# Batch 3's mirrored rows of the second transform read backwards from the same PSUM banks, their residual and output rows reversed through DRAM

## The chip, the core and the metric

The kernel runs on one core of one Trainium2 chip. The metric is the device time of one execution in microseconds. The core has five instruction streams that run side by side and wait for each other by semaphores: TensorE (PE, matrix products into eight PSUM banks), VectorE (DVE), ScalarE (ACT), GpSimd (POOL) and SyncE (SP), which issues most of the transfers. Transfers run on 16 DMA engines.

## The reference

Two layers after one another. The first is a linear attention with decay, step by step over 768 positions; the second mixes the result with a two-dimensional Fourier transform and puts a normalised two-layer network behind it.

```python
# attention, per batch and head: state (48 x 48)
y[t]  = r[t] @ (state + u * k[t] v[t]^T)
state = w[t] * state + k[t] v[t]^T
# x: (4, 768, 384), heads side by side
X  = fft(fft(x, axis=1), axis=2)
u  = x + real(X)
un = (u - mean(u)) / sqrt(var(u) + 1e-6)
out = u + relu(un @ w_ch1) @ w_ch2        # 384 -> 1536 -> 384
```

## The kernel before, in words

There are four batches, each of six chunks of 128 positions. The work of a batch has two parts.

`attention(b, c)` handles a chunk. Four inputs (w, k, r, v) come in 192 KB loads with seven buffers each; the logarithm of w is summed by two products (L773, L777), r and k are scaled, transposed (on TensorE for the first 18 chunks, by a DMA transposition for batch 3), multiplied (L843), masked on VectorE (L848), and the product with v and the state (L893) gives the chunk's rows `x`, which VectorE adds up at L908 into `X`. `fold(b, c)` adds and subtracts mirrored chunks and columns, for the first transform.

`mix(b)` holds the rest. The first transform is done with cosine and sine tables in three products (j = 0, 2, 1; 24 short matmuls of 193 columns from batch 1 on, L968), whose results are moved to `HCS`. Since a real transform is symmetric, only positions 0 to 384 stand in `HCS`; `HCR` (L976 to L983) is a copy of it, reversed and with signs, for positions 385 to 767. The second transform (L989 to L993) makes six blocks `kb` of 128 rows and 384 columns: three matmuls a block, blocks 0 to 2 with weights from `HCS`, blocks 3 to 5 from `HCR`, all against the table `DTM`. VectorE adds the residual `x` and sums the rows (L997) into `UF`; ScalarE or VectorE writes the shifted rows `UN`, ScalarE sums their squares for the variance. For batches 2 and 3 a DMA transposition, issued by SyncE (L1033), turns three blocks of `UN` into `UNT`, one transposition for each half `hf` of a batch (blocks 0 to 2, blocks 3 to 5).

The network then runs half by half: twelve first-layer tiles (three matmuls of 384 columns, L1056) with a relu on ScalarE or VectorE into `HT`, then for each block three second-layer groups of four matmuls (L1075). VectorE scales by the deviation and adds `UF` (L1081) into one of three buffers `OSB`, and SyncE writes it to the output (L1085). The last block of the last batch is cut into 256 and 128 columns, so that its end is short.

The order of the work is written out by hand: `ORDER` holds for each engine the list of operation numbers in which it works, and with them also which engine does an operation that could run on several. Each engine works strictly in its list's order; an operation that waits holds up all behind it on its engine. That is true of SyncE too, whose waits precede its transfers. `schedule` gives each tile its PSUM bank from the lists; `emit` derives the semaphore waits. Numbers such as 1252 or 1299 below are these operation numbers; 1252 is the last attention product of batch 3 in both kernels. Operations below 1259 are the same in both; those of batch 3's `mix` are numbered anew. TensorE's list has 36 matmuls without use (L1130) in the first 37 us.

Of the kernel before, what the change touches and what calls it, by code (L numbers as in the profile page):

```python
# [7 lines left out]
ALU = mybir.AluOpType  # L8
# [28 lines left out]
MEANS = (0, 1, 2, 3)  # L37
# [29 lines left out]
    "act": (  # L67
# [14 lines left out]
    "dve": (  # L82
# [14 lines left out]
    "pool": (  # L97
# [12 lines left out]
}  # L110


class _Tile:


    __slots__ = ("bank", "ops", "pool", "n_done", "end")
# [1047 lines left out]
```

## Time and profile before

| | us |
|---|---|
| median of three runs | 183.09 (182.17 to 183.48) |
| the profiled execution | 184.21 |
| its span, first to last instruction | 182.4 |
| TensorE busy in it | 176.8 |
| VectorE, ScalarE, GpSimd busy | 148.2, 130.2, 101.5 |

The granted clock of TensorE is 1.000 in the whole span. Busy times of TensorE overlap: a 384-column matmul is shown with about 326 ns, while the next one can begin half of that later, so its share of busy time says little of how much of it is used. The chain of waits (what released the work that ended last, step by step) shows the real pitch. A row of the timeline gives the start, the duration, the engine, the line, the operation, the tile written and those read, and in brackets how long the engine had been idle and who released it. A row of waits gives the sum, the count and the longest. The rows of DMA groups give the size and the time from issue to landing. In the rows of "DMA" and "GB/s" a stretch is cut into 40 slices; a digit is the mean busy share of the 16 engines in tenths.

### The profile page before, as it was taken

The page shows a single profiled execution, that of the slowest core. Times are in us where ns is not written, and L with a number is a line of the kernel's source. Part 1 is how long each engine was busy: PE and PEld are TensorE (multiplying, and loading weights), DVE is VectorE, ACT ScalarE, POOL GpSimd, SP SyncE. Part 2 cuts the span into 40 slices and gives each one's busy share as a digit, 9 for nine tenths or more (in the row PEclk, how much of TensorE's full clock was granted, in tenths as well). Part 3 has the DMA queues.
Part 4 walks back from the last instruction along what each step waited for, and adds up shares of the span by engine and source line. Part 5 has one row for each costly group of instructions (what it writes and reads, how often), then busy time and mean ns, then how long its engine had stood idle before and what let it go on. Part 6 is the DMA issues. An engine that isn't in the chain of part 4 may idle for free.

```text
span 182.4 us, 4568 instructions
## 1 busy us (share of the span) xinstructions
PE 176.8 (97%) x1722; PEld 116.3 (64%) x1722; DVE 148.2 (81%) x341; ACT 130.2 (71%) x340; POOL 101.5 (56%) x120
## 2 busy tenths in 40 slices
PE   7999999999999999999999999999999999999994
PEld 3465676766566666776657666656666676666663
DVE  8779999899899999999888997899979927622343
ACT  2889859597898675799899978888882247478200
POOL 2448789767231498589998968769653440000000
DMA  4999998999999899999999999997550103331214
GB/s 97 203 216 196 208 191 172 185 202 208 152 196 190 162 210 230 226 204 182 202 222 218 219 177 207 220 212 179 103 114 0 47 2 65 73 125 43 86 71 145
DMA packets 116119, 28.99 MB, mean 159 GB/s; under 512 B 111361, under 2 KB 116098, under 8 KB 116098
## 3 DMA queue, kind: packets, MB, share of 16 engines
q1 hardware_dynamic: 114514, 26.36, 70.2%
q0 software_dynamic: 1584, 2.36, 8.0%
q8 instruction: 13, 0.21, 0.5%
q14 instruction: 8, 0.07, 0.1%
HBM read 23.59 MB, written 4.72 MB: 155 GB/s over the span
## 4 chain that ended last, share of the span: by engine, by line
PE 61%; DVE 17%; DMA 9%; SPq 4%; ACT 4%; issue 3%; DVEq 0%
PE bank L1075 18%; PE bank L1056 17%; DMA in_w<-in_w_dram 5%; DMA w<-in_moe_w_ch_dram 4%; DVE ah L848 4%; SPq L609 4%; PE bank L992 3%; PE bank L1130 3%; PE bank L1098 3%; PE bank L968 3%; DVE osb L1081 2%; PE bank L843 2%; DVE rkh L561 2%; PE bank L889 2%; PE bank L899 2%
## 5 line engine op out<-in xcount | busy, mean ns | idle before, releaser
L1075 PE MATMUL bank<-w,ht 128*128 128x384 bf16 (+2 forms) x300 | 53.7, 320 | 0.0
L1056 PE MATMUL bank<-unt,w 128*128 128x384 bf16 x288 | 51.9, 326 | 0.6 <-DMA w<-in_moe_w_ch_dram 0.6
L1064 ACT ACTIVATE ht<-bank 128x384 bf16<-128x384 f32 x72 | 32.6, 496 | 9.3 <-PE bank L1056 8.9
L1056 PEld LDWEIGHTS bank<-unt,w 128*128 128x128 bf16 x288 | 26.9, 98 | 17.5 <-DVE ht L1062 0.8
L1075 PEld LDWEIGHTS bank<-w,ht 128*128 128x128 bf16 x300 | 27.5, 98 | 15.2
L848 DVE TENSOR_TENSOR ah<-bank,msk 128x512 bf16<-128x512 f32 x48 | 31.2, 682 | 2.1 <-PE bank L843 2.0
L561 POOL TENSOR_TENSOR rk<-rk,ub 128x384 f32<-128x384 f32 x21 | 21.6, 1034 | 8.6 <-DVE rk L561 7.0
L561 POOL TENSOR_TENSOR vtd<-in_v,dc 128x384 f32<-128x384 f32 x20 | 16.7, 837 | 11.2 <-DVE dc L800 8.1
L1081 DVE SCALAR_TENSOR_TENSOR osb<-bank,rstd,uf 128x384 f32<-128x384 f32 (+2 forms) x25 | 14.8, 596 | 9.5 <-PE bank L1075 5.9
L1062 DVE TENSOR_SCALAR ht<-bank 128x384 bf16<-128x384 f32 x24 | 13.0, 549 | 6.9 <-PE bank L1056 6.8
L561 POOL TENSOR_TENSOR rk<-in_r,in_k 128x384 f32<-128x384 f32 x17 | 16.9, 999 | 2.9 <-DMA in_r<-in_r_dram 1.4
L997 DVE SCALAR_TENSOR_TENSOR uf<-bank,x 128x384 f32<-128x384 f32 x24 | 12.5, 553 | 4.7 <-PE bank L992 4.6
L561 POOL TENSOR_TENSOR rkh<-in_k,e 128x384 bf16<-128x384 f32 x14 | 14.1, 1009 | 3.6 <-ACT e L792 2.0
L779 ACT ACTIVATE bank<-bank 128x384 f32<-128x384 f32 x24 | 11.5, 484 | 5.8 <-PE bank L773 5.8
L811 DVE TENSOR_TENSOR rkh<-bank,in_r 128x384 bf16<-128x384 f32 x24 | 13.1, 549 | 2.1 <-ACT bank L779 2.0
L575 ACT ACTIVATE xf<-uf,agg 128x384 bf16<-128x384 f32 x24 | 14.7, 614 | 0.0
L561 POOL TENSOR_TENSOR xf<-sd 128x382 bf16<-128x382 f32 (+1 forms) x10 | 10.6, 1062 | 6.5 <-DVE sd L561 3.0
L575 ACT ACTIVATE lb<-in_w 128x384 bf16<-128x384 f32 x24 | 12.4, 519 | 2.1 <-DMA in_w<-in_w_dram 1.8
L575 ACT ACTIVATE un<-uf,agg 128x384 bf16<-128x384 f32 x18 | 10.6, 611 | 4.1 <-DVE uf L997 4.1
L586 ACT ACTIVATE rkt<-bank 128x256 f32<-128x256 f32 x29 | 10.8, 389 | 3.6 <-PE bank L833 2.4
L561 POOL TENSOR_TENSOR sd<-x 128x385 f32<-128x385 f32 x10 | 10.0, 1015 | 5.9 <-DVE x L908 5.4
L792 ACT ACTIVATE e<-bank 128x392 f32<-128x392 f32 (+1 forms) x24 | 11.7, 497 | 2.3 <-DVE bank L877 1.0
(138 smaller groups left out, 358.7 us busy)
## 6 DMA issues: line engine op xcount, KB each, us to landing
in_w<-in_w_dram SPq DMA_DIRECT2D x24, 192.0 KB, 3.8
in_k<-in_k_dram SPq DMA_DIRECT2D x24, 192.0 KB, 3.8
in_r<-in_r_dram SPq DMA_DIRECT2D x24, 192.0 KB, 4.1
in_v<-in_v_dram SPq DMA_DIRECT2D x24, 192.0 KB, 4.0
out_dram<-osb SPq DMA_DIRECT2D x23, 192.0 KB, 2.8
w<-in_moe_w_ch_dram POOLq DMA_DIRECT2D x2, 576.0 KB, 8.1
w<-in_moe_w_ch_dram POOLq DMA_DIRECT2D x1, 1152.0 KB, 10.7
out_dram<-osb SPq DMA_DIRECT2D x1, 128.0 KB, 1.7
```

Of the source, the lines that this page charges most:

```text
L561: return lambda e: e.tensor_tensor(out=o, in0=a, in1=b, op=f)
L575: return lambda e: e.activation(o, a, f, **kw)
L779: op("act", a_ps(DM) + 20, lambda e: e.activation(ps(tce)[:, 0:DM], ps(tce)[:, 0:DM], ACTF.Exp), w=[tce])
L792: op("act", a_ps(ne), lambda e: e.activation(E2[i2][:, 0:ne], ps(tci)[:, 0:ne], ACTF.Exp), r=[tci], w=[("E2", i2)])
L811: op("dve", v_1(DM), lambda e: e.tensor_tensor(out=rh[:, :, 0:D], in0=ps(tce)[:, 0:DM].rearrange("t (h d) -> t h d", d=D), in1=rt[:, :, :] ...
L848: masked[n] = op("dve", v_1(512), lambda e, x=x: e.tensor_tensor(out=ah[:, x:H:2, :], in0=ps(ta[x])[:, :].rearrange("p (h t) -> p h t", t= ...
L997: op("dve", v_1(DM) + 60, lambda e, kb=kb, t=t: e.scalar_tensor_tensor(out=uf[:, kb, :], in0=ps(t)[:, 0:DM], scalar=1.0, in1=xb[:, kb, 0:D ...
L1056: ins = e.matmul(ps(t)[:, 0:384], W1[:, m, 256 * (j // 2) + j % 2:256 * (j // 2) + 256:2], unt[:, :, m, :], start=(m == 0), stop=(m == NM ...
L1062: {"dve": lambda e, j=j, t=t, ht=ht: e.tensor_scalar(out=ht[:, j, :], in0=ps(t)[:, 0:384], scalar1=su, scalar2=0.0, op0=ALU.mult, op1=ALU. ...
L1064: "act": lambda e, j=j, t=t, ht=ht: e.activation(ht[:, j, :], ps(t)[:, 0:384], ACTF.Relu, scale=su)},
L1075: ins = e.matmul(ps(t)[:, 0:hi - lo], ht[:, j, 128 * x:128 * x + 128], W2[:, j, lo:hi], start=(j == 0), stop=(j == NJ - 1))
L1081: op("dve", v_1(hi - lo) + 64, lambda e, kb=kb, t=t, o=o, lo=lo, hi=hi: e.scalar_tensor_tensor(out=o[:, lo:hi], in0=ps(t)[:, 0:hi - lo], s ...
```

## The change

For batch 3 (`MIRROR = (3,)`) no `HCR` is made and blocks 3 to 5 have no matmuls of their own. The tile of block 0 serves block 3 too, that of block 1 block 4, that of block 2 block 5: VectorE reads the bank a second time with the columns backwards (384 to 1). `DTM` and the tiles are one column wider for this (385). The rows come out in mirrored order of positions, so two things are reversed through DRAM:

- The residual rows of chunks 3 to 5 are written to a scratch tensor `XD` in DRAM (four transfers, each chunk twice, one copy behind the other) and read back in reversed row order into `UF` (three transfers, 192 KB each). The addition for blocks 3 to 5 then takes `UF` in place of `x`.
- The output rows of blocks 3 to 5 go from `OSB` to a scratch tensor `OD` in two pieces, swapped, and from there in reversed row order to the output (a third transfer each, DRAM to DRAM). Two single rows go out by themselves.

Position 384, which has no mirror, is made by two matmuls with one column of weights and an addition on one partition, into row 0 of block 3.

The blocks are taken in the order 0, 3, 1, 4, 2, 5, and the network does the second half (blocks 3 to 5) first in its numbering, with the buffers `UN` and `UNT` swapped accordingly. All five lists of `ORDER` are new, for all batches. In TensorE's list four first-layer tiles of half 0 come ahead of those of half 1; in VectorE's list operation 1299 (block 3's addition) comes ahead of the other additions of batch 3; the last block on TensorE is block 1, uncut; the cut block is block 2. In `load_one` only the planned cost of a load is altered. The branch for kernels without `MEANS`, which no batch took, is gone.

Core of the diff:

```diff
+MIRROR = (3,)
...
+    def move(fn, r, w, sem, xfer):
+        op("sp", 620, fn, r=r, w=w, sem=sem, xfer=xfer, dma=(1150, 600))
+
+    def back(x, a):
+        return x[a - 63:a + 577, :].rearrange("(z p) d -> z p d", z=2)[:, 63::-1, :]
...
-        for kb in range(NC):
+        if b in MIRROR:
+            xd = XD[b][0:S, :].rearrange("(z c p) d -> z p c d", p=128, z=2)
+            for z in range(2):
+                move(lambda e, z=z: e.dma_start(xd[z, :, 0:2, :], xb[:, 3:5, 0:DM]), [("X", i, 3), ("X", i, 4)], [("XD", b, z, 0)],
+                     "xa%d%d" % (i, z), 1040)
+                move(lambda e, z=z: e.dma_start(xd[z, :, 2, :], xb[:, 5, 0:DM]), [("X", i, 5)], [("XD", b, z, 1)], "xb%d%d" % (i, z), 520)
+            for q in (1, 2, 0):
+                move(lambda e, q=q: e.dma_start(uf[:, NP + q, :], back(XD[b], 384 - 128 * q)),
+                     [("XD", b, z, y) for z in range(2) for y in range(2)], [("UF", i, NP + q)], "xz%d" % q, 520)
+        for kb in (0, 3, 1, 4, 2, 5) if b in MIRROR else range(NC):
...
+            op("dve", v_1(DM) + 60, lambda e, kb=kb, t=t, flip=flip: e.scalar_tensor_tensor(
+                out=uf[:, kb, :], in0=ps(t)[:, DM:0:-1] if flip else ps(t)[:, 0:DM], scalar=1.0,
+                in1=uf[:, kb, :] if flip else xb[:, kb, 0:DM], op0=ALU.mult, op1=ALU.add,
+                accum_out=agg[:, kb, 0:1]), r=[t, ("UF" if flip else "X", i, kb)], w=[("UF", i, kb), ("SUM", i, kb)])
...
+                    move(lambda e, o=o, od=od, m=m, nh=nh: e.dma_start(od[0:nh, :], o[m:m + nh, :]), done, [("OD", b, mq, 0)],
+                         "oa%d" % (n % 3), 260)
+                    move(lambda e, o=o, od=od, m=m, nh=nh: e.dma_start(od[nh:2 * nh, :], o[m - nh:m, :]), done, [("OD", b, mq, 1)],
+                         "ob%d" % (n % 3), 260)
...
+                    t0 = S - 127 - 128 * mq
+                    move(lambda e, od=od, nh=nh, t0=t0: e.dma_start(
+                        out[b, t0:t0 + 2 * nh, :].rearrange("(z p) d -> z p d", z=2),
+                        od[0:2 * nh, :].rearrange("(z p) d -> z p d", z=2)[:, ::-1, :]),
+                         [("OD", b, mq, 0), ("OD", b, mq, 1)], [("out", b, kb, 0)], "fin%d" % mq, 1040)
```

Here `nh` is 63 for block 3 and 64 for blocks 4 and 5.

More of the change, by code (lines that the diff above doesn't have):

```diff
@@ L292, in schedule @@
                 hw.append([s + o.set, o.xfer, o, t])
-                if o.xfer == 960:
+                if o.xfer in (920, 1030):
                     lds.append(o)
@@ L395, in run @@
                 for s in dcount:
-                    if s.startswith("out"):
+                    if s[:3] in ("out", "fin", "oc0", "oc1"):
                         eng.wait_ge(sems[s], dcount[s])
@@ L492, in bass_rwkv6_finch__then__fnet_fourier_mix_kernel @@
     UF = [sb("uf%d" % i, [NC, DM], FP32) for i in range(2)]
-    BST = [sb("bst%d" % i, [6], FP32) for i in range(4)]
     AGG = [sb("agg%d" % i, [NC, 2], FP32) for i in range(2)]
@@ L506, in bass_rwkv6_finch__then__fnet_fourier_mix_kernel @@
     SS = sb("ss", [NP, 2 * HE], BF16)
+    XD = {b: nc.dram_tensor("xd%d" % b, (1024, DM), FP32, kind="Internal").ap() for b in MIRROR}
+    OD = {b: nc.dram_tensor("od%d" % b, (S - S // 2, DM), FP32, kind="Internal").ap() for b in MIRROR}
     CN = sb("cn", [NP, HE], BF16)
     SN = sb("sn", [NP, HE], BF16)
-    DTM = sb("dtm", [3, DM], BF16)
+    DTM = sb("dtm", [3, DM + 2], BF16)
     IDW = sb("idw", [384], BF16)
@@ L734, in rows @@
                         idn = (IDW if cos or half else NIDW)[p0:p0 + np_, 128 - sh:256 - sh]
-                        src = tab[:, 0:HE] if half == 0 else tab[:, HE - 2:0:-1]
-                        dst = ps(t)[:, 0:HE] if half == 0 else ps(t)[:, HE:DM]
+                        src = tab[:, 0:HE] if half == 0 else tab[:, HE - 2::-1]
+                        dst = ps(t)[:, 0:HE] if half == 0 else ps(t)[:, HE:DM + 1]
                         ins = e.matmul(dst, idn, src, start=(i == 0), stop=(i == len(moves[j]) - 1))
@@ L984, in mix @@
         agg, lnv, rstd = AGG[i], LNV[i], RSTD[i]
-        su = -1.0 / DM if b in MEANS else -1.0
-        for kb in range(NC):
-            n = b * NC + kb
-            t = g.tile("f")
-            for j in range(3):
-                def f(e, j=j, kb=kb, t=t):
-                    a = 128 * (kb % NP)
-                    return e.matmul(ps(t)[:, 0:DM], (hcs if kb < NP else HCR)[:, j, a:a + 128], DTM[:, j, :], start=(j == 0), stop=(j == 2))
-                op("pe", mm(DM), f, r=[("HCS" if kb < NP else "HCR", j), "DTM%d" % j], w=[t])
-            iu = (2 * b + kb // 3) % len(UN)
-            un = UN[iu][:, kb % 3, :]
-            if b in MEANS:
-                op("dve", v_1(DM) + 60, lambda e, kb=kb, t=t: e.scalar_tensor_tensor(
-                    out=uf[:, kb, :], in0=ps(t)[:, 0:DM], scalar=1.0, in1=xb[:, kb, 0:DM], op0=ALU.mult, op1=ALU.add,
-                    accum_out=agg[:, kb, 0:1]), r=[t, ("X", i, kb)], w=[("UF", i, kb), ("SUM", i, kb)])
-                op(None, {"act": a_sb(DM) + 95, "dve": v_2(DM) + 60},
-                   {"act": act(un, uf[:, kb, :], ACTF.Identity, scale=-float(DM), bias=agg[:, kb, 0:1]),
-                    "dve": ts(un, uf[:, kb, :], -float(DM), agg[:, kb, 0:1], ALU.mult, ALU.add)}, port=("dve",),
-                   r=[("UF", i, kb), ("SUM", i, kb)], w=[("UN", iu, kb % 3)])
-                op("act", a_sb(DM) + 190, act(xf[:, kb, 63:447], uf[:, kb, :], ACTF.Square, scale=-float(DM), bias=agg[:, kb, 0:1],
-                                              accum_out=agg[:, kb, 1:2]),
-                   r=[("UF", i, kb), ("SUM", i, kb)], w=[("AGG", i, kb)] + [(z, i, kb) for z in ("XFe", "XFo", "XFn")])
-            else:
-                op("dve", v_1(DM), lambda e, kb=kb, t=t: e.tensor_tensor(
-                    out=uf[:, kb, :], in0=ps(t)[:, 0:DM], in1=xb[:, kb, 0:DM], op=ALU.add),
-                   r=[t, ("X", i, kb)], w=[("UF", i, kb)])
-                bs = BST[n % 4]
-                op("dve", v_1(DM), lambda e, kb=kb, bs=bs: e.bn_stats(bs[:, :], uf[:, kb, :]),
-                   r=[("UF", i, kb)], w=[("BST", n % 4)])
-                op("dve", 89, lambda e, kb=kb, bs=bs: e.bn_aggr(agg[:, kb, :], bs[:, :]),
-                   r=[("BST", n % 4)], w=[("AGG", i, kb)])
-                op(None, {"act": a_sb(DM) + 95, "dve": v_2(DM) + 60},
-                   {"act": act(un, uf[:, kb, :], ACTF.Identity, scale=-1.0, bias=agg[:, kb, 0:1]),
-                    "dve": ts(un, uf[:, kb, :], agg[:, kb, 0:1], -1.0, ALU.subtract, ALU.mult)}, port=("dve",),
-                   r=[("UF", i, kb), ("AGG", i, kb)], w=[("UN", iu, kb % 3)])
@@ new lines, in mix @@
+        su = -1.0 / DM
+        made = {}
+        place = {x: 1 - x if b in MIRROR else x for x in range(2)}
+        if b in MIRROR:
+            xd = XD[b][0:S, :].rearrange("(z c p) d -> z p c d", p=128, z=2)
[6 more added lines that the diff above has]
+                     [("XD", b, z, y) for z in range(2) for y in range(2)], [("UF", i, NP + q)], "xz%d" % q, 520)
@@ new lines, in mix, with f @@
+        for kb in (0, 3, 1, 4, 2, 5) if b in MIRROR else range(NC):
+            n = b * NC + kb
+            flip = b in MIRROR and kb >= NP
+            if not flip:
+                t = made[kb] = g.tile("f")
+                for j in range(3):
+                    def f(e, j=j, kb=kb, t=t, w=DM + (b in MIRROR)):
+                        a = 128 * (kb % NP)
+                        return e.matmul(ps(t)[:, 0:w], (hcs if kb < NP else HCR)[:, j, a:a + 128], DTM[:, j, 0:w],
+                                        start=(j == 0), stop=(j == 2))
+                    op("pe", mm(DM), f, r=[("HCS" if kb < NP else "HCR", j), "DTM%d" % j], w=[t])
+            t = made[kb % NP if flip else kb]
+            iu = (2 * b + place[kb // 3]) % len(UN)
+            un = UN[iu][:, kb % 3, :]
+            op("dve", v_1(DM) + 60, lambda e, kb=kb, t=t, flip=flip: e.scalar_tensor_tensor(
+                out=uf[:, kb, :], in0=ps(t)[:, DM:0:-1] if flip else ps(t)[:, 0:DM], scalar=1.0,
+                in1=uf[:, kb, :] if flip else xb[:, kb, 0:DM], op0=ALU.mult, op1=ALU.add,
+                accum_out=agg[:, kb, 0:1]), r=[t, ("UF" if flip else "X", i, kb)], w=[("UF", i, kb), ("SUM", i, kb)])
+            if flip and kb == NP:
+                t = g.tile("f")
+                def f(e, t=t):
+                    for j in range(2):
+                        ins = e.matmul(ps(t)[0:1, 0:DM], hcs[:, j, DM:DM + 1], DTM[:, j, 0:DM], start=(j == 0), stop=(j == 1))
+                    return ins
+                op("pe", mm(DM, 2), f, r=[("HCS", j) for j in range(2)] + ["DTM%d" % j for j in range(2)], w=[t])
+                op("dve", v_1(DM) + 60, lambda e, kb=kb, t=t: e.scalar_tensor_tensor(
+                    out=uf[0:1, kb, :], in0=ps(t)[0:1, 0:DM], scalar=1.0, in1=xb[0:1, kb, 0:DM], op0=ALU.mult, op1=ALU.add,
+                    accum_out=agg[0:1, kb, 0:1]), r=[t, ("X", i, kb)], w=[("UF", i, kb), ("SUM", i, kb)])
+            op(None, {"act": a_sb(DM) + 95, "dve": v_2(DM) + 60},
+               {"act": act(un, uf[:, kb, :], ACTF.Identity, scale=-float(DM), bias=agg[:, kb, 0:1]),
+                "dve": ts(un, uf[:, kb, :], -float(DM), agg[:, kb, 0:1], ALU.mult, ALU.add)}, port=("dve",),
+               r=[("UF", i, kb), ("SUM", i, kb)], w=[("UN", iu, kb % 3)])
+            op("act", a_sb(DM) + 190, act(xf[:, kb, 63:447], uf[:, kb, :], ACTF.Square, scale=-float(DM), bias=agg[:, kb, 0:1],
+                                          accum_out=agg[:, kb, 1:2]),
+               r=[("UF", i, kb), ("SUM", i, kb)], w=[("AGG", i, kb)] + [(z, i, kb) for z in ("XFe", "XFo", "XFn")])
@@ L1020, in mix @@
             hf = kb // 3
-            unt = UNT[(2 * b + hf) % 2]
+            unt = UNT[(2 * b + place[hf]) % 2]
             if b < DMA_U:
@@ L1069, in mix @@
                 o = OSB[n % 3]
-                for lo, hi in ((0, DM),) if n < B * NC - 1 else ((0, 256), (256, DM)):
+                for lo, hi in ((0, DM),) if (b, hf, x) != (B - 1, 0 if b in MIRROR else 1, 2) else ((0, 256), (256, DM)):
                     t = g.tile("f")
@@ L1084, in mix @@
                        r=[t, ("RSTD", i, hf), ("UF", i, kb)], w=[("OSB", n % 3, lo)] + ([] if lo else [("OSB", n % 3, 256)]))
-                    op("sp", 620, lambda e, kb=kb, o=o, lo=lo, hi=hi: e.dma_start(
-                        out[b, kb * 128:(kb + 1) * 128, lo:hi], o[:, lo:hi]),
-                       r=[("OSB", n % 3, lo)], w=[("out", b, kb, lo)], sem="out%d" % (n % 3), xfer=520, dma=(1150, 600))
+                    if b not in MIRROR or kb < NP:
+                        move(lambda e, kb=kb, o=o, lo=lo, hi=hi: e.dma_start(out[b, kb * 128:(kb + 1) * 128, lo:hi], o[:, lo:hi]),
+                             [("OSB", n % 3, lo)], [("out", b, kb, lo)], "out%d" % (n % 3), 520)
+                        continue
+                    mq = kb - NP
+                    m = 65 if mq == 0 else 64
+                    nh = 63 if mq == 0 else 64
+                    od = OD[b][128 * mq:128 * mq + 128, :]
+                    done = [("OSB", n % 3, 0)]
+                    move(lambda e, o=o, od=od, m=m, nh=nh: e.dma_start(od[0:nh, :], o[m:m + nh, :]), done, [("OD", b, mq, 0)],
+                         "oa%d" % (n % 3), 260)
+                    move(lambda e, o=o, od=od, m=m, nh=nh: e.dma_start(od[nh:2 * nh, :], o[m - nh:m, :]), done, [("OD", b, mq, 1)],
+                         "ob%d" % (n % 3), 260)
+                    if mq == 0:
+                        move(lambda e, o=o: e.dma_start(out[b, S - 1:S, :], o[1:2, :]), done, [("out", b, S - 1)], "oc0", 30)
+                        move(lambda e, o=o: e.dma_start(out[b, S // 2:S // 2 + 1, :], o[0:1, :]), done, [("out", b, S // 2)],
+                             "oc1", 30)
+                    t0 = S - 127 - 128 * mq
[3 more added lines that the diff above has]
+                         [("OD", b, mq, 0), ("OD", b, mq, 1)], [("out", b, kb, 0)], "fin%d" % mq, 1040)
     g.ctx = "begin"
```

26 lines of the change are left out of this document (11 added, 15 removed), and 128 rows, old and new, of the table ORDER.

## The prediction

> **What bounds the kernel now.** I read the page first, then what TensorE waits for, then the chain that ended last, then the stretch from 138 us to the end in order of time, and last the DMA views of the quiet stretches.
>
> ```profile
> span 182.4 us, 4568 instructions
> ...
> PE 176.8 (97%) x1722; PEld 116.3 (64%) x1722; DVE 148.2 (81%) x341; ACT 130.2 (71%) x340; POOL 101.5 (56%) x120
> ...
> DMA  4999998999999899999999999997550103331214
> ```
>
> ```profile
> PE bank L1098 <- DVE w L572: 1.3, 1, 1.3
> PE bank L1056 <- DMA w<-in_moe_w_ch_dram: 0.6, 1, 0.6
> PE bank L777 <- ACT ht L1064: 0.3, 1, 0.3
> PE bank L833 <- POOL rkh L561: 0.3, 1, 0.3
> PE bank L843 <- ACT ht L1064: 0.2, 1, 0.2
> ```
>
> TensorE waits 2.7 us in all, 1.3 of it before its first instruction. The DMA engines are full for two thirds of the span and nearly idle in the last third. From the chain come the real costs of matmuls, which overlap:
>
> ```profile
> 146.27 0.84 PE bank L968 x10
> ...
> 156.38 7.80 PE bank L1056 x48
> 164.18 0.65 PE bank L1075 x4
> ...
> 173.28 6.54 PE bank L1075 x52
> 179.92 0.35 DVE osb L1081
> ```
>
> A 384-column matmul costs 7.80/48 = 0.1625 us, a group of four 0.65, a first-layer tile (three) 0.49, a 193-column one 0.084. After the last attention product of batch 3 (operation 1252, done at 141.9) the order of before holds 25 first-layer tiles (12.2), 29 second-layer groups (18.85), 18 matmuls of the second transform (2.9), 23 short ones (1.9) and the last block, cut in two (2.0): 37.85 us. 141.9 + 37.85 = 179.8, which is where TensorE stops. So the tail is matmuls end to end: each one removed is time, and each wait put in front of them is time too.
>
> **The removed work.** Nine 384-column matmuls (blocks 3 to 5 of batch 3) go, two come for the one row without a mirror: -7 x 0.1625 = -1.14 us. The lists say where: after 1252 the new order holds one first-layer tile more, one short matmul less and seven 384-column matmuls less: 37.1 us, so -0.73 there and -0.41 earlier. The extra column (385 for 384) is 0.0004 us a matmul. The three reversed copies of batch 3 fall away:
>
> ```profile
> 142.57 0.54 DVE L908 TENSOR_TENSOR x<-bank,vtd 128x384 f32<-128x384 f32 x1
> ...
> 144.14 0.34 SPq L1085 DMA_DIRECT2D out_dram<-osb  x1
> ...
> 144.78 0.55 DVE L561 TENSOR_TENSOR sd<-x 128x385 f32<-128x385 f32 x1
> ...
> 149.09 1.25 POOL L565 TENSOR_SCALAR hcr<-hcs,cp 128x384 bf16<-128x384 bf16 x1 [2.01 <-ACT hcs L586]
> 149.28 0.52 ACT L978 ACTIVATE hcr<-hcs 128x384 bf16<-128x384 bf16 x1
> ...
> 149.92 0.56 DVE L997 SCALAR_TENSOR_TENSOR uf<-bank,x 128x384 f32<-128x384 f32 x1 [3.46 <-PE bank L992]
> 150.40 0.08 DVE L997 DVE_READ_ACCUMULATOR uf<-bank,x 128x1 f32 x1
> 150.41 0.56 DVE L997 SCALAR_TENSOR_TENSOR uf<-bank,x 128x384 f32<-128x384 f32 x1
> ...
> 152.13 6.02 SPq L1033 DMA_TRANSPOSE unt<-un  x2
> ...
> 153.93 0.75 DVE L566 TENSOR_SCALAR un<-uf,agg 128x384 bf16<-128x384 f32 x2
> ```
>
> They run beside matmuls of batch 2, so they count nothing; without that cover the one on GpSimd, 1.25, would have stood in front of blocks 3 to 5. A residual addition (the operation at L997) starts every 0.48 us; reading its bank backwards I take at the same price, since the nearest row with a reversed operand (the fold, L561, 0.55) costs what the straight ones do.
>
> **The new path in the middle.** Residual rows 3 to 5 now go to DRAM and come back reversed. The last, x of chunk 5, is written at 143.1. SyncE then issues two writes of it (0.34 each), waits until they land, and issues three back-reads; behind them in its queue stand an output and both transposes of the normalised rows. On VectorE the first operation that needs a back-read (1299) stands in front of every residual addition and of the normalised rows 0 to 4. So the back-reads gate both transposes, and these gate the first layer of batch 3. Without delay VectorE gets to 1299 at 143.1 + five fold operations (2.5) + six evictions and output rows (3.1): 148.7. From there: four additions, one normalising (0.37), one addition, one normalising: 151.9, first transposition; one addition, one normalising, the row without a mirror (0.48), one normalising: 153.6, second one.
>
> ```profile
> L1033 SPq DMA_TRANSPOSE unt<-un x2: 1278/1284/1289, 152.1 to 156.9; - x2
> ...
> DMA to landing us min/median/max: 3.2/3.2/3.3
> ```
>
> They land at 155.1 and 156.8. TensorE has its other work until 179.15 - 23.4 = 155.75, takes four first-layer tiles of half 0 (1.95), and turns to half 1 at 157.7. The cover is 0.65 and 0.9 us: any lateness of the back-reads beyond that shows in full. The banks of blocks 0 to 2 stay taken until the mirrored addition has read them; with the lists' five other open tiles that is eight, so TensorE gets through batch 2's groups. SyncE issues 24 transfers for batch 3 instead of 9, 15 x 0.34 = 5.1 us, where it had nothing to do; that counts only if one stands ahead of a late one.
>
> **What a back-read costs.** No transfer of before looks like it: all those of 192 KB have 128 rows in their outermost loop. `back` and the final reversal `fin` have two blocks of 64 (63) rows there, each walked backwards. What 192 KB of 1536-byte rows cost in a quiet stretch:
>
> ```profile
> DMA  9993000000000000000000000000000379999982
> GB/s 389 328 369 123 21 0 0 0 0 0 0 0 0 0 0 0 0 0 0 0 0 0 0 0 0 0 0 0 0 0 0 123 266 348 328 369 430 369 307 82
> ...
> out_dram<-osb SPq DMA_DIRECT2D x1, 192.0 KB, 1.9
> ```
>
> ```profile
> 170.00:176.00 6.00, 6.00 (x40) 3.67 (x38) 1.85 (x5) 0.00 (x0) 0.00 (x0) 1.00 0.28 98
> ```
>
> Data flow for about 0.6 us of the 1.9: some 0.8 lie before, 0.4 behind. Three such outputs in 170 to 176 take 0.28 x 6 = 1.68 us of all 16 engines, 0.56 each, 350 GB/s; the best slice shows 430. Bounds for one back-read: all 16 engines, 0.56 us; one engine, 9 us. If the work is dealt out by the outermost loop, a loop of two feeds two engines: 196,608 bytes at 2/16 of 430 to 350 GB/s is 3.66 to 4.48 us, middle 4.03. I take this value: of all that the code shows, the count of two is what sets these transfers apart from the rows quoted, and both blocks lie on one queue with nothing else to divide by.
>
> The Trainium skill, "DMA: Bandwidth & Descriptors", section "Why a DMA increments its semaphore by 16 and not by 1", states the same rule: the engine count is the largest number up to 16 that divides the outermost counts of both sides, and the lowest-numbered engines are used. By it each of these transfers runs on two engines and all on the same two, and the sum would be the one below; by the rows of the ordinary outputs alone it would be 182.5. No run here shows it yet.
>
> **The sum.** Back-reads: writes issued at 143.2 and 143.6, landed at 145.5; first back-read issued 145.6, data 146.4 to 150.4, landed 150.85; the other two on the same engines at 154.9 and 158.9. VectorE: 1299 at 150.85; three waiting additions; 1322 at 154.9; then normalise, add, normalise: 156.6, first transposition, landed 160.0. 1310 at 158.9, then 0.37, 0.48 and 0.37 with its own 0.5: 160.7, second transposition, landed 164.0. TensorE stands from 155.75 to 160.0, works 1.95 us, stands until 164.0, and has 23.4 - 1.95 = 21.5 us left: its end is 185.5, 6.35 later than without the wait.
>
> Then the end. By the new order blocks 3, 5, 4 (in this order on SyncE) are finished 10.1, 7.7 and 5.65 us before TensorE stops; each goes to DRAM in two pieces and from there backwards to the output. The first `fin` is issued about 6.1 us before the stop (SyncE takes block 5's pieces ahead of it), 179.4, data from 180.2; three at 4.03 on the same two engines: 192.3. The ordinary outputs issued behind them need those engines too, three blocks of 0.5: 193.8, landed 194.2.
>
> ```profile
> 178.38 0.62 DVE L1081 SCALAR_TENSOR_TENSOR osb<-bank,rstd,uf 128x384 f32<-128x384 f32 x1 [0.68 <-PE bank L1075]
> ...
> 179.92 0.35 DVE L1081 SCALAR_TENSOR_TENSOR osb<-bank,rstd,uf 128x128 f32<-128x128 f32 x1 [0.19 <-PE bank L1075]
> ```
>
> ```profile
> in_w<-in_w_dram SPq DMA_DIRECT2D x24, 192.0 KB, 3.8
> ...
> out_dram<-osb SPq DMA_DIRECT2D x1, 64.0 KB, 1.6
> ```
>
> Before, the last piece was 128 columns wide, issued at 180.3, landed 181.9, and the span ended 0.5 later. So the new span is 194.7, +12.3. Without slow transfers the new end would still lose 0.55 us: its last block is whole, 0.27 more on VectorE and 0.3 more to land (1.9 for 1.6).
>
> The profiled execution took 184.21 us, 1.8 outside its span; +12.3 makes 196.5. The median is 183.09, 1.1 below that execution, so 195.4, and I forecast 195.5. With 3.66 us a transfer it is 193.1, with 4.48 it is 198.4.
>
> **The new order elsewhere.** All five lists are rearranged; before batch 3's transform the same operations run. Some 30 elementwise operations go from GpSimd to VectorE and 27 back, and the loads swap places, two of chunk 5 (k and r) behind a transposition of chunk 3. Against the rows this can win at most what TensorE now waits beyond its start, 1.4 us, and I take the same as the loss: nothing as the value, 1.4 both ways in the range. It would be hidden by the batch-2 matmuls that wait beside attention; if they run out, the operation after 1252 moves by the whole delay.
>
> **Rivals.** First, and on the other side: the transfers use all 16 engines, or enough of them. The first back-read then lands at 147.5, the others by 148.6, ahead of 148.7; even with the 3.8 us that loads take on a full queue it is 149.4, which the cover holds within 0.1. The reversals at the end land near the stop of TensorE, under the last output. What is left is -1.14 + 0.55 = -0.6: 182.5. It decides from about eight engines on, 1.1 us a transfer. For it speaks that every 192 KB row here is spread wide; against it the outer count. Second: two engines each, but different ones, so that three run side by side. They land from 150.85 to 151.75, the chain is 2.15 late, 1.5 after the cover; the last reversal, issued 2.5 before the stop, lands 2.75 behind it, against 2.6 for the last output. -0.6 + 1.5 + 0.2: 184.2. Nothing in the rows speaks for a rotation of engines. Third, the worst: DRAM to DRAM is slower than SBUF to DRAM; at twice the data time the end grows by 12 more, past 205.
>
> **How the numbers follow.** Same two engines 0.70 (195.5, own range 190 to 203: 3.66 to 4.48 us, 1.4 of order, and the cover or a slower DRAM reversal); different pairs 0.08 (184.2); wide 0.18 (182.5); worse 0.04. From 184.0 to 203.0 the first two are held, 0.78, and the rest is left out. 1% is about what a measurement of this kernel can tell from no change (the three runs spread over 0.7%): 181.3 and 184.9. Faster 0.04 from the wide case with a lucky order, within 0.22 (most of the wide case and the different pairs), slower 0.74.
>
> **What would show it.** The landing time of the back-reads: about 5, 9 and 13 us for the three if they share two engines, 2 if not. A DMA share near 0.12 (2 of 16) from 146 to 159 and again through the end. TensorE's wait on the transposed rows, some 6 us in two pieces between 155 and 164. An end in which TensorE has stopped and SyncE's reversals still run for 8 us. The forecast is wrong if the share in these stretches rises above a half, or if VectorE's 1299 starts near 148.7 with no wait; then what is left is the first rival.

## The result and the profile after

After the change the kernel takes 199.74 us (median of four runs, 199.34 to 200.34), before it 182.8 (four runs). The ratio is 1.093, 95% interval 1.088 to 1.098: slower by 9%. The profiled execution after took 199.5 us with a span of 197.7.

The page of the kernel after, with the slices that answer to those of before:

```profile
span 197.7 us, 4600 instructions
...
PE 178.0 (90%) x1715; PEld 115.5 (58%) x1715; DVE 152.6 (77%) x357; ACT 125.6 (64%) x327; POOL 96.8 (49%) x116
...
PEclk9999999999999999999999999999999957999965
DMA  5999999999998999899995999890502353103123
```

TensorE's busy time grew by 1.2 us although seven matmuls fell away: the clock row dips in slices 33 and 34 (158 to 168 us), where the kernel before has none, and once more at the very end. Now the waits of TensorE and of VectorE (sum, count, longest):

```profile
PE bank L1074 <- DMA unt<-un: 6.0, 1, 6.0
```

```profile
DVE uf L1020 <- DMA uf<-xd: 9.0, 3, 4.3
...
DVE osb L1099 <- DMA out_dram<-osb: 8.6, 2, 8.2
```

TensorE has one new wait, for the transposed rows of batch 3. VectorE waits three times for back-reads and, at the end, 8.2 us for an output buffer. The kernel before has no wait of the first two kinds, and waits 1.2 us in all for output buffers. The middle in order of time (L915 is x of a chunk, L1002 its write to DRAM, L1004 the back-reads, L1020 the residual addition, L1055 the transposition, L1074 the first layer):

```profile
139.73 0.56 DVE L915 TENSOR_TENSOR x<-bank,vtd 128x384 f32<-128x384 f32 x1 [0.45 <-POOL xf L562]
140.32 1.45 SPq L1002 DMA_DIRECT2D xd<-x  x2
143.37 3.07 SPq L1004 DMA_DIRECT2D uf<-xd  x3
149.81 3.74 PE L1093 MATMUL bank<-w,ht 128*128 128x384 bf16 x22
150.01 0.56 DVE L1020 SCALAR_TENSOR_TENSOR uf<-bank,uf 128x384 f32<-128x384 f32 x1 [4.33 <-DMA uf<-xd]
154.00 0.56 DVE L1020 SCALAR_TENSOR_TENSOR uf<-bank,uf 128x384 f32<-128x384 f32 x1 [2.46 <-DMA uf<-xd]
155.90 5.40 SPq L1055 DMA_TRANSPOSE unt<-un  x2
157.99 0.56 DVE L1020 SCALAR_TENSOR_TENSOR uf<-bank,uf 128x384 f32<-128x384 f32 x1 [2.17 <-DMA uf<-xd]
159.60 11.90 PE L1074 MATMUL bank<-unt,w 128*128 128x384 bf16 x54 [6.05 <-DMA unt<-un]
```

The three additions that need a back-read start 3.99 us apart: that is what one back-read takes. TensorE runs dry at 149.81 + 3.74 = 153.55 and starts again at 159.60, when the first transposition has landed. The windows of this stretch (busy times of the engines, then granted clock, DMA share, GB/s):

```profile
147.00:150.00 3.00, 3.00 (x20) 1.49 (x18) 0.00 (x0) 0.49 (x1) 0.00 (x0) 1.00 0.13 49
...
158.00:160.00 2.00, 0.40 (x2) 0.24 (x3) 1.93 (x7) 0.00 (x0) 0.00 (x0) 0.70 0.40 86
160.00:162.00 2.00, 2.00 (x8) 0.95 (x7) 0.98 (x2) 0.26 (x1) 0.00 (x0) 0.50 0.43 84
...
166.00:168.00 2.00, 2.00 (x14) 1.22 (x13) 0.00 (x0) 1.34 (x4) 0.00 (x0) 1.00 0.00 0
```

While a back-read runs alone, the DMA share is 0.13 at 49 GB/s: that is the share of two of 16 engines. And the granted clock is halved from about 158.8 to 165.6, just where TensorE starts again: 8 matmuls in 2 us at 160, 14 at 166. The end (L1121 is the reversal to the output, L1118 a single row of 1.5 KB, L1104 an ordinary output):

```profile
178.81 7.34 PE L1093 MATMUL bank<-w,ht 128*128 128x384 bf16 x56
180.50 0.69 SPq L1121 DMA_DIRECT2D out_dram<-od  x1
182.47 0.66 SPq L1121 DMA_DIRECT2D out_dram<-od  x1
183.17 1.04 SPq L1118 DMA_DIRECT2D out_dram<-osb  x1
187.92 0.65 SPq L1121 DMA_DIRECT2D out_dram<-od  x1
188.61 4.80 SPq L1104 DMA_DIRECT2D out_dram<-osb  x4
191.91 1.14 DVE L1099 SCALAR_TENSOR_TENSOR osb<-bank,rstd,uf 128x384 f32<-128x384 f32 x2 [8.16 <-DMA out_dram<-osb]
```

```profile
184.00:187.00 3.00, 2.16 (x14) 1.08 (x11) 0.00 (x0) 0.00 (x0) 0.00 (x0) 1.00 0.12 45
```

TensorE stops at 186.15 (before: 179.81), and the span ends 11.55 us later (before: 2.59). So the 15.3 us between the two spans are 6.3 ahead of TensorE's stop and 9.0 behind it. Behind the stop two engines are again the sign: from 185.5 to 196.5 the DMA share never falls below 0.13.

### The profile page after: what moved, and what is told of

It is laid out like the page before. It is cut to its first block, busy times and chain, and to the rows that moved or that the text cites. A ratio compares the mean times of both kernels' runs of the same rounds, so it can differ in the third digit from the quotient of the medians.

```text
span 197.7 us, 4600 instructions
## 1 busy us (share of the span) xinstructions
PE 178.0 (90%) x1715; PEld 115.5 (58%) x1715; DVE 152.6 (77%) x357; ACT 125.6 (64%) x327; POOL 96.8 (49%) x116
## 4 chain that ended last, share of the span: by engine, by line
PE 60%; DMA 15%; DVE 8%; SPq 7%; issue 3%; ACT 2%; POOL 1%; POOLq 1%; DVEq 0%
PE bank L1074 21%; PE bank L1093 15%; SPq L610 5%; DMA uf<-xd 5%; PE bank L1014 4%; DMA out_dram<-osb 4%; PE bank L975 3%; PE bank L850 3%; DMA in_w<-in_w_dram 3%; DMA unt<-un 2%; DVE ah L855 2%; PE bank L906 2%; PE bank L834 2%; PE bank L784 1%; PE bank L780 1%
## 5 line engine op out<-in xcount | busy, mean ns | idle before, releaser
L1074 PE MATMUL bank<-unt,w 128*128 128x384 bf16 x288 | 57.0, 339 | 6.1 <-DMA unt<-un 6.0
L1082 ACT ACTIVATE ht<-bank 128x384 bf16<-128x384 f32 x68 | 31.4, 492 | 20.1 <-PE bank L1074 19.6
L1074 PEld LDWEIGHTS bank<-unt,w 128*128 128x128 bf16 x288 | 27.3, 101 | 24.4 <-DMA unt<-un 6.4
L1093 PEld LDWEIGHTS bank<-w,ht 128*128 128x128 bf16 x300 | 27.5, 98 | 15.3 <-issue 0.3
L562 POOL TENSOR_TENSOR rkh<-in_k,e 128x384 bf16<-128x384 f32 x17 | 17.2, 1012 | 11.6 <-ACT e L799 7.8
L562 POOL TENSOR_TENSOR rk<-rk,ub 128x384 f32<-128x384 f32 x20 | 20.4, 1025 | 4.6 <-DVE rk L562 4.5
L1080 DVE TENSOR_SCALAR ht<-bank 128x384 bf16<-128x384 f32 x28 | 14.9, 551 | 9.1 <-PE bank L1074 8.8
L562 POOL TENSOR_TENSOR vtd<-in_v,dc 128x384 f32<-128x384 f32 x21 | 17.3, 830 | 7.5 <-DVE dc L807 5.5
L807 DVE TENSOR_REDUCE dc<-rk 128x8 f32<-128x384 f32 x24 | 13.1, 545 | 0.2 <-POOL rk L562 0.2
L562 POOL TENSOR_TENSOR xf<-sd 128x382 bf16<-128x382 f32 (+1 forms) x9 | 9.1, 1021 | 7.2 <-DVE sd L562 5.4
L915 DVE TENSOR_TENSOR x<-bank,vtd 128x384 f32<-128x384 f32 x19 | 10.4, 552 | 2.1 <-PE bank L906 1.7
L576 ACT ACTIVATE vb<-in_v 128x384 bf16<-128x384 f32 x23 | 11.9, 526 | 0.0
```

What stands on the lines that cost most here:

```text
L562: return lambda e: e.tensor_tensor(out=o, in0=a, in1=b, op=f)
L576: return lambda e: e.activation(o, a, f, **kw)
L807: op("dve", v_1(DM), lambda e: e.tensor_reduce(out=dc[:, :], in_=rku[:, :, :], axis=mybir.AxisListType.X, op=ALU.add), r=[("RK", i2)], w=[ ...
L1074: ins = e.matmul(ps(t)[:, 0:384], W1[:, m, 256 * (j // 2) + j % 2:256 * (j // 2) + 256:2], unt[:, :, m, :], start=(m == 0), stop=(m == NM ...
L1080: {"dve": lambda e, j=j, t=t, ht=ht: e.tensor_scalar(out=ht[:, j, :], in0=ps(t)[:, 0:384], scalar1=su, scalar2=0.0, op0=ALU.mult, op1=ALU. ...
L1082: "act": lambda e, j=j, t=t, ht=ht: e.activation(ht[:, j, :], ps(t)[:, 0:384], ACTF.Relu, scale=su)},
```

## The experiments

The theory is the prediction's: transfers with two blocks outermost run on two engines, 4.0 us each; the back-reads then starve TensorE, the reversals lengthen the end. The rivals: it is the backward walk, or DRAM as source and destination, that is slow; or the loss lies in the new order. Executions differ by up to 2.7 us in when VectorE starts on x of chunk 5 (139.7 to 142.4, but for one told below). So single executions are compared from an event inside them where fractions matter.

**Each path made wide, and both.** The rows are not reversed here, only moved in 128 plain rows.

```diff
 def back(x, a):            # back_wide
+    return x[a - 127:a + 1, :]
...
 # fin_wide
-    out[b, t0:t0 + 2 * nh, :].rearrange("(z p) d -> z p d", z=2),
-    od[0:2 * nh, :].rearrange("(z p) d -> z p d", z=2)[:, ::-1, :]
+    out[b, t0:t0 + 2 * nh, :], od[0:2 * nh, :]
```

> The back-reads take 128 rows forwards in one loop, so blocks 3 to 5 get residual rows in the wrong order; the final reversals stay. Both theories (count, direction): back-reads land about 2 us after issue, TensorE's wait of 6.05 us and the 2.85 us that the half clock costs behind it go, the end stays as long: 199.7 - 8.9 = 190.8. If the round trip through DRAM itself is too long for the cover, a wait of 1 us or more for the transposed rows stays and the time is above 192.

> The final copies from the scratch tensor to the output go forwards in one piece, so the output rows of blocks 3 to 5 of batch 3 are in the wrong order; the back-reads stay. If the two engines set the end: TensorE stops where it did (about 186.1), and the 11.6 us behind the stop shrink to about 3.1: 199.7 - 8.5 = 191.2. If the output's path over DRAM (two transfers after one another) sets it, at least 3 us of the 8.5 stay.

> Both of the above: back-reads and final copies forwards and wide, so rows of blocks 3 to 5 are in the wrong order on both ways; all else as in the changed kernel. By the two-engine theory nothing of the loss remains: 199.7 - 8.9 - 8.5 = 182.3, level with the kernel before (182.8). By a theory in which the mirrored reads, the queue order or the new order cost something of their own, it stays above 184.5.

Measured, one execution each: 191.1 with wide back-reads, 191.75 with wide reversals. With both 182.53 (10 runs) against 182.8 before (13 runs), ratio 0.998, interval 0.993 to 1.002. Taken away alone, the back-reads are thus worth 199.74 - 191.1 = 8.6 and the reversals 8.0, to within what single executions differ; both together are worth 199.74 - 182.53 = 17.2. With both wide:

```profile
140.21 0.56 DVE L915 TENSOR_TENSOR x<-bank,vtd 128x384 f32<-128x384 f32 x1 [0.45 <-POOL xf L562]
...
146.46 0.56 DVE L1020 SCALAR_TENSOR_TENSOR uf<-bank,uf 128x384 f32<-128x384 f32 x1 [0.31 <-PE bank L1014]
...
147.90 0.55 DVE L1020 SCALAR_TENSOR_TENSOR uf<-bank,uf 128x384 f32<-128x384 f32 x1
...
149.93 0.55 DVE L1020 SCALAR_TENSOR_TENSOR uf<-bank,uf 128x384 f32<-128x384 f32 x1
...
153.87 8.94 PE L1074 MATMUL bank<-unt,w 128*128 128x384 bf16 x54
...
170.12 7.34 PE L1093 MATMUL bank<-w,ht 128*128 128x384 bf16 x56
```

No addition waits for a back-read, TensorE does not wait for transposed rows, its 54 first-layer matmuls take 8.94 us instead of 11.90, and it stops at 177.46. The span, 180.6, ends 3.1 later. All the rest of the change (order, added transfers, buffers, mirrored additions), taken together, is worth nothing that this measurement can tell.

**Count or direction.** Two blocks outermost, walked forwards, so the residual rows are not reversed:

```diff
 def back(x, a):            # two_forward, two_forward_again
+    return x[a - 63:a + 577, :].rearrange("(z p) d -> z p d", z=2)[:, 0:64, :]
```

> The back-reads keep their two blocks in the outermost loop, but each block is walked forwards, so blocks 3 to 5 get residual rows in the wrong order. If the outermost count of two is what costs (two of sixteen engines): the three back-reads still land 4.0 us apart, VectorE still waits about 9 us for them, TensorE still stands 6 us and the time is 199.7 within 1. If walking backwards is what costs: they land about 2 us after their issue, TensorE's wait and the half clock behind it are gone, 190.8.

The first execution took 207.67, because a load of r came 4.8 us late at 57.6 us and everything behind it was later (VectorE starts on x of chunk 5 at 147.3); the additions already stood 4.00 apart in it. So it was run again:

> The kernel with two forward blocks of 64 rows outermost in the back-reads once more (residual rows of batch 3 in the wrong order), since the first execution was delayed 7.5 us by a late load ahead of the attention. If the count of two and not the direction sets the price, additions that wait for back-reads again stand 4.0 us apart and the time is 199 to 201, as after the change; if the direction did, they are 1 us or less apart and the time is near 191.

It took 200.69, beside a kernel before of 185.02 on that chip:

```profile
152.00 0.56 DVE L1020 SCALAR_TENSOR_TENSOR uf<-bank,uf 128x384 f32<-128x384 f32 x1 [4.85 <-DMA uf<-xd]
155.99 0.56 DVE L1020 SCALAR_TENSOR_TENSOR uf<-bank,uf 128x384 f32<-128x384 f32 x1 [2.47 <-DMA uf<-xd]
159.99 0.56 DVE L1020 SCALAR_TENSOR_TENSOR uf<-bank,uf 128x384 f32<-128x384 f32 x1 [2.17 <-DMA uf<-xd]
```

4.0 us apart, forwards as backwards: the direction costs the back-reads nothing, the count sets the price. Four blocks outermost should then halve it, but need four copies of the residual rows in DRAM:

```diff
 def back(x, a):            # four_blocks
+    return x[a - 31:a + 1377, :].rearrange("(z p) d -> z p d", z=4)[:, 31::-1, :]
...
-            for z in range(2):
+            for z in range(4):
```

> Four blocks of 32 rows in the outermost loop of the back-reads instead of two of 64 (each still backwards; four copies of the residual rows in the scratch tensor, so four more writes). If the outermost count sets the number of engines, each back-read takes 2.0 us instead of 4.0: VectorE's additions for blocks 3, 5, 4 come 2.0 us apart, TensorE's wait falls from 6.05 to about 1.5 us, too short for the half clock: 199.7 - 4.5 - 2.85 = 192.4. If a backward transfer has a fixed low rate, they stay 4.0 apart and the time is 199.7 or more.

Measured 198.27, against 192.4 expected:

```profile
141.24 3.33 SPq L1002 DMA_DIRECT2D xd<-x  x4
147.50 1.80 SPq L1004 DMA_DIRECT2D uf<-xd  x3
...
152.59 0.56 DVE L1020 SCALAR_TENSOR_TENSOR uf<-bank,uf 128x384 f32<-128x384 f32 x1 [6.00 <-DMA uf<-xd]
154.52 0.56 DVE L1020 SCALAR_TENSOR_TENSOR uf<-bank,uf 128x384 f32<-128x384 f32 x1 [0.41 <-DMA uf<-xd]
156.50 0.56 DVE L1020 SCALAR_TENSOR_TENSOR uf<-bank,uf 128x384 f32<-128x384 f32 x1 [0.16 <-DMA uf<-xd]
```

1.93 and 1.98 us apart, half of 4.0: the price goes by the count. My time missed the extra writes. They took SyncE 3.3 us instead of 1.45, and the first back-read was issued 6.3 us behind the write instead of 3.05. TensorE still waited 5.3 us.

**Which engines.** The back-reads and reversals go to GpSimd's queue, everything else stays:

```diff
-    move(..., "xz%d" % q, 520)          # and "fin%d", on SyncE
+    move(..., "xz%d" % q, 520, eng="pool")
```

> The three back-reads and the three final reversals are issued by GpSimd, which has nothing to do by then, instead of SyncE; access patterns unchanged. If the shortage is that three transfers of one queue share the same two engines, and GpSimd's transfers take other pairs in turn: the back-reads run side by side and land 5 to 7 us after issue, TensorE's wait falls to 2 us, the half clock goes, and the last output no longer stands behind the reversals: 183 to 187. If they land on the same two engines: 199. If GpSimd's transfers use all sixteen: 182.5.

Measured 196.85 (4 runs), ratio 1.077 (1.068 to 1.085), not the 183 to 187 expected. The three additions and one window:

```profile
152.57 0.56 DVE L1019 SCALAR_TENSOR_TENSOR uf<-bank,uf 128x384 f32<-128x384 f32 x1 [6.39 <-DMA uf<-xd]
154.01 0.55 DVE L1019 SCALAR_TENSOR_TENSOR uf<-bank,uf 128x384 f32<-128x384 f32 x1
155.75 0.55 DVE L1019 SCALAR_TENSOR_TENSOR uf<-bank,uf 128x384 f32<-128x384 f32 x1
```

```profile
147.00:153.00 6.00, 6.00 (x38) 3.31 (x36) 0.43 (x1) 0.49 (x1) 0.21 (x1) 1.00 0.42 123
```

Only the first addition waits, and the share is 0.42 at 123 GB/s: the three run side by side, on different engines. But each lands 7.8 us after its issue (144.71 to 152.57 for the first), more than the 6.6 of SyncE's first. What is gained by running side by side is lost to this longer landing: TensorE's wait is 5.1 us for 6.0, and the clock halves again. The end is still 9.4 us behind TensorE's stop. The Trainium skill, "DMA: Bandwidth & Descriptors", section "Why a DMA increments its semaphore by 16 and not by 1", states that hardware queues use the lowest-numbered engines, while GpSimd's software queue takes consecutive engines from a cursor that moves on. The traces agree as far as they go: one after another at 49 GB/s on SyncE's queue, side by side at 123 on GpSimd's; the numbers of the engines they do not show.

**The halved clock.** 40 matmuls without use fill the gap in TensorE's list:

```diff
+    for _ in range(40):     # gap_filled, ahead of batch 3's first layer
+        e.matmul(ps(tz)[:, 0:384], MSK[:, :], IDW[:, :])
```

> 40 matmuls without use (6.5 us) stand in TensorE's list between the last work of batch 2 and the first layer of batch 3, where it waits. If the wait of 6 us is what halves the clock behind it: the clock stays 1.0, the 54 first-layer matmuls behind the wait take 8.8 instead of 11.9 us, the filler itself costs about 0.4, so 197.3. If the clock falls for another reason, or the end hangs on transfers alone: 199.7 or 200.1.

```profile
154.85 6.66 PE L1174 MATMUL bank<-idw,msk 128*128 128x384 bf16 x40
165.37 6.99 PE L1076 MATMUL bank<-unt,w 128*128 128x384 bf16 x42 [1.68 <-DMA unt<-un]
...
179.67 7.34 PE L1095 MATMUL bank<-w,ht 128*128 128x384 bf16 x56
```

The clock stays at 1.00 until TensorE's stop, so the halving follows from TensorE standing idle. Yet this execution took 200.41, not 197.3. Its first back-read came 1.98 us later than after the change (151.99 for 150.01). And a second wait of 1.68 us showed, for the second transposition. From the first waiting addition to TensorE's stop it is 35.0 us for 36.1: the clock's 3.0 us are won, about 1.7 of them are given back to that wait. A single execution with a margin of 1 us: the sign is shown, the size only roughly.

**The held buffer at the end.** VectorE's wait of 8.16 us ends when the single row of 1.5 KB lands. Here that row is issued ahead of the reversals:

```diff
-    1374 1359 1367 1418      # SyncE's list, oc_early
+    1359 ... 1374 1367 1418
```

> The single row that is issued between the second and the third reversal (1.5 KB, which landed 8.6 us later and held an output buffer of VectorE) is issued with the other single row, ahead of the reversals. Its landing should fall to about 2 us and VectorE's 8.2 us wait for the buffer should go. If the backlog on two engines sets the end, the time stays within 1 of 199.7, since the outputs still stand behind the last reversal there. If the held buffer sets it, the outputs leave 5 us earlier: 194.5.

```profile
180.09 7.34 PE L1093 MATMUL bank<-w,ht 128*128 128x384 bf16 x56
```

Measured 200.89; VectorE's long wait is gone (one of 2.4, for another buffer, is left), but the span, 199.1, ends 11.67 us behind TensorE's stop at 187.43, as before that edit (11.55). The held buffer is a symptom. The last outputs are issued 2.8 us sooner after the stop, and then wait for the two engines: the share is 0.13 to 0.15 from 193 to 198.

**Reversed, but wide.** The same reversal, digit by digit: a first move reverses the rows inside blocks of 8 with 16 blocks outermost, a second reverses the blocks with the 8 outermost.

```diff
+    # residual: SBUF to XD, XD to XE, then 128 plain rows into UF (one hop more)
+    xd[c, :, ::-1, :], xb[:, 3 + c, 0:DM]
+    xe[2 - c, :, ::-1, :], xs[c, :, :, :]
+    uf[:, NP + q, :], XE[b][128 * q:128 * q + 128, :]
...
+    # output: OSB to OD, OD to out
+    od[0:nr, :].rearrange("(z s) d -> z s d", s=ns)[:, ::-1, :], o[f0:f0 + nr, :]
+    out[b, t0:t0 + nr, :].rearrange("(z s) d -> s z d", s=ns)[:, ::-1, :], od[0:nr, :].rearrange("(z s) d -> s z d", s=ns)
```

> The rows are still reversed through DRAM, but digit by digit, so that no large transfer has two blocks outermost: the residual rows go from SBUF to DRAM with 16 blocks of 8 outermost and each block walked backwards, from DRAM to DRAM with 8 outermost and the 16 blocks walked backwards, and come to SBUF in 128 plain rows; each output block is written once, with 16 (14) blocks of 8 (9) walked backwards, and goes from DRAM to the output with the blocks walked backwards. If the outermost count alone made the transfers slow, each 192 KB back-read and each final reversal lands within about 2.5 to 3 us at a DMA share well above 0.13, VectorE waits less than 1.5 us for back-reads, TensorE does not wait for transposed rows, and the time is that of the kernel with wide transfers and unreversed rows, 182.5, plus 0 to 0.8 for the extra hop through DRAM: 182.5 to 183.3. If it is the walking backwards through DRAM, or DRAM-to-DRAM transfers, that are slow, all six stay near 4 us and the time stays above 190.

Measured 190.3 (4 runs) against 185.02 before on that chip, ratio 1.026 (1.020 to 1.032):

```profile
141.59 0.57 SPq L1003 DMA_DIRECT2D xd<-x  x1
145.08 0.35 SPq L1008 DMA_DIRECT2D uf<-xe  x1
145.52 0.63 SPq L1006 DMA_DIRECT2D xe<-xd  x1
149.31 0.80 SPq L1008 DMA_DIRECT2D uf<-xe  x2
...
151.88 0.56 DVE L1024 SCALAR_TENSOR_TENSOR uf<-bank,uf 128x384 f32<-128x384 f32 x1 [4.95 <-DMA uf<-xe]
153.32 0.55 DVE L1024 SCALAR_TENSOR_TENSOR uf<-bank,uf 128x384 f32<-128x384 f32 x1
...
158.56 9.65 PE L1078 MATMUL bank<-unt,w 128*128 128x384 bf16 x42 [3.75 <-DMA unt<-un]
```

Backward walks and DRAM to DRAM at full width cost no 4 us: once the first has landed, no addition waits, and the end is 3.9 us behind TensorE's stop instead of 11.55. That part held, and some 70% of the loss (2.6% for 9.3%) is gone with the rows still reversed. My 182.5 to 183.3 failed on the hops. The write, the reversal and the read stand one behind the other, 3.9, 3.8 and 2.6 us from issue to the next issue or the addition. The first addition, at 151.88, is 5.4 later than with wide transfers. Of this 0.8 is the later x of chunk 5; the other 4.6 are the longer way through DRAM, for which I had allowed 0.8. TensorE waits 3.75 us, and the halved clock takes another 2.8 (42 matmuls in 9.65 us, 6.83 at 0.1625). 0.8 + 3.75 + 2.8 = 7.35 is what TensorE's stop lies behind that of the kernel with wide transfers.

The same with the last block cut in two again:

```diff
-    1371 1393 1364 1414 1365 ... 1401 1405 1406    # TensorE's list, two_steps_cut
+    1371 1393 1364 1365 1399 ... 1414 1415 1416
```

> As the kernel with the reversal in two steps, and the last block in the order of TensorE, VectorE and SyncE is again the one that is computed and written in two pieces, as before the change. If the whole last block is what was left of the loss, TensorE's stop to the end of the span is 2.5 us instead of 3.1 and the time is 0.55 less than without the cut: 182.0, which is 0.995 to 1.000 of the kernel before. If the end is set by the final reversals instead, the cut changes nothing.

Measured 191.18 (6 runs), ratio 1.032 (1.027 to 1.036): the cut regained nothing. TensorE stops at 185.09. From 179.9 on VectorE waits 5.5 us for the output buffer that the single row holds, so its last evictions start only at 185.41, and the span ends at 189.7, 4.6 behind the stop. In this kernel the end hangs on that buffer, held while the row stands behind the reversals, and not on the size of the last block.

## Why the prediction came out as it did

The forecast was 195.5; 199.74 is 4.2 more, and inside the range of 184 to 203, which was wide because it held the second rival too. The mechanism was right: two engines for each transfer, the same two, a starved TensorE and a long end. Two of the hits in its numbers are luck, and one cost was not on the list. Measured against the kernel with wide transfers (span 180.6), the 17.1 us are 8.7 ahead of TensorE's stop and 8.4 behind it.

- **The price of a two-block transfer**, 4.03 forecast: right, 4.0 us, at a share of 0.13 and 49 GB/s. The choice between the bounds went by the count of two; two forward blocks and four blocks show that the count is it. By the rule of the Trainium skill cited in the prediction it had to be two engines, the same ones: the trace agrees.
- **The fixed part of a back-read**, 0.8 before and 0.4 behind: wrong. The first takes 6.64 us from issue to addition, 2.6 beside the 4.0. Its data flow only from about 145.5, 2.1 us after the issue at 143.37; with wide transfers they flow from 144.5, 0.7 after the issue at 143.83. Why two blocks start later is left open. The forecast for the write ahead of it was short by 0.6 too: 3.05 us to the first back-read, forecast 2.4. So from x of chunk 5 to the first addition it is 9.7 us instead of 7.75. That the landing came out all the same (150.01 for 150.85) is luck: x of chunk 5 was ready 2.8 us earlier than in the execution that the forecast was counted from.
- **TensorE's wait**, 6.35 us in two pieces, 4.25 and 2.05: the sum is right by luck, the shape is not. It is one wait of 6.05. The first piece is longer, since the back-reads start later than forecast while TensorE ran dry at 153.55, not at 155.75; and the second does not show.
- **The second piece** is hidden by a cost that I had not on the list: the halved clock. The 54 first-layer matmuls take 11.90 us instead of 8.94, 3.0 more, and meanwhile the second transposition lands. With the clock kept up the piece shows as 1.7. Ahead of the stop it is 8.7 for the 6.35 forecast: 5.7 are the later start of the first layer (159.60 for 153.87) and 3.0 are the clock.
- **The end**, 9.2 us behind TensorE's stop (194.7 for 185.5): wrong in size, 11.55. Three reversals in a row on the same two engines are right, and the loss of 8.0 that wide reversals take away shows it. By the sum the two engines were through 8.3 us behind the stop (193.8); in the trace they work on until 196.8, 10.7 behind. Of these 2.4 us, 0.45 are the issue of the first reversal, 5.65 us ahead of the stop instead of 6.1. The rest was not measured apart; the sum left out the shares of the 96 KB pieces on the two engines, and took 0.8 us from issue to data, where the back-reads took 2.1. The third reversal has to wait for its own pieces, and is issued 6.7 us behind the first of them (2.8 with wide reversals). But that leaves no gap in the share of 0.13, so it does not explain the size.
- **The uncut last block**, 0.55: it fits where nothing else covers it. With wide transfers the end is 3.14 us behind the stop, before 2.59, so 0.55. No run cuts the block in that kernel.
- **Matmuls removed (-1.14), copies of HCR, reversed bank reads, new order**: right as a sum, as far as can be told. The first rival, all engines, was forecast at 182.5, and that kernel takes 182.53; it differs from before by no more than the interval. The reversed reads start the next operation 0.48 us later, like straight ones. The single terms were not measured apart.
- **The rivals**: different pairs of engines, 184.2, had the wrong price: on GpSimd's queue the transfers do run side by side, but take 7.8 us to land. DRAM to DRAM at twice the time did not occur: in the long end the rate is 45 to 49 GB/s, as in the back-reads.

## What to carry to other kernels

Before data take a way through DRAM to be reordered, look at the outermost count of the access pattern: it sets how many engines share a transfer, and a DMA share of 0.13 in a quiet stretch is the sign. Split the reordering so that every move has 8 or 16 outermost, but count the hops as well: each cost 2.6 to 3.9 us here, and two of them fitted the cover where three did not. And when a new wait starves TensorE for some microseconds, add what the clock takes afterwards: 1.3 to 3.0 us in the runs here, whose waits were 3.6 to 6.7 us.

## What the runs showed of the hardware

- The granted clock halved 5.3 us after TensorE ran dry in the kernel after (dry at 153.55, halved at 158.8), 2.4 us in the kernel with two steps (154.8, 157.2), 2.6 us in the second run with two forward blocks (155.0, 157.6). It stayed halved for 6.8 us (after, 158.8 to 165.6) or 3.4 us (two steps with the cut, 159.9 to 163.3). It cost 3.0 us where TensorE worked in that time, and nothing where it still waited. The Trainium skill, "TensorE: Matmul & The Clock Gate", Part 1, states a free-running window of about 3.4 us that decides on the clock, with one idle window before it halves. The halved stretches of one and of two such windows agree; a halving after 2.4 or 2.6 us without a matmul does not agree with a whole idle window, so a mostly idle one seems to be enough.
- A row of 1.5 KB took 8.62 us to land, issued at 183.17 behind the reversals, and held up VectorE's last two evictions through the buffer it came from. The last long step in the chain of waits of the kernel after is this row, though moving it ahead did not shorten the end:

```profile
183.17 8.62 DMA out_dram<-osb
```

- On GpSimd's queue the two-block back-reads took 7.8 us from issue to landing while three ran side by side. Such a transfer takes 4.0 us on SyncE's queue beside its start; what fills the rest here is left open.
